# A new order of all steps, 29 copies and residual sums on another engine, and new buffers in a four-layer attention kernel

## The chip, the cores and the metric

The kernel runs on one core of a Trainium2 chip. The metric is the device time of one execution in microseconds. A core has five engines that run side by side, each through its own list of instructions in order: PE (TensorE, matmuls, with the weight loads shown apart as PEld), DVE (VectorE), ACT (ScalarE), POOL (GpSimd) and SP (SyncE, which here issues nearly all transfers). An instruction waits until what it reads is written and until the buffer that it writes is free.

## The reference

A residual stream x of 2048 x 512 (bf16) goes through four layers, A, B, A, B. The two A layers share their weights, and so do the two B layers. 32 heads of 16.

```python
def _A_ref(x, wqkv, w_phi, wo):
    q, k, v = qkv[0], qkv[1], qkv[2]              # qkv = x @ wqkv, by head
    pq = jnp.einsum("bhsd,hdf->bhsf", q, w_phi)
    pk = jnp.einsum("bhsd,hdf->bhsf", k, w_phi)
    phi_q = jnp.concatenate([_softmax(pq), _softmax(-pq)], axis=-1)
    phi_k = jnp.concatenate([_softmax(pk), _softmax(-pk)], axis=-1)
    kv = jnp.einsum("bhsf,bhsd->bhfd", phi_k, v)
    z  = jnp.einsum("bhsf->bhf", phi_k)
    num = jnp.einsum("bhqf,bhfd->bhqd", phi_q, kv)
    den = jnp.einsum("bhqf,bhf->bhq", phi_q, z)[..., None] + 1e-6
    return merge_heads(num / den) @ wo

def _B_ref(x, wqkv, wo):                          # W, dil = 8, 2
    idx = pos[:, None] - off[None, :]             # off = 0, 2, .. 14
    logits = jnp.einsum("bhsd,bhswd->bhsw", q, kg) * scale   # kg, vg: k, v at idx
    logits = jnp.where(mask, logits, -1e9)        # mask = idx >= 0
    return merge_heads(einsum(softmax(logits), vg)) @ wo

x = x + _A_ref(_layernorm(x), A_wqkv, A_w_phi, A_wo)
x = x + _B_ref(_layernorm(x), B_wqkv, B_wo)
x = x + _A_ref(_layernorm(x), A_wqkv, A_w_phi, A_wo)
x = x + _B_ref(_layernorm(x), B_wqkv, B_wo)
```

## The kernel before

x stays on the core as four blocks (x0 to x3) of 512 rows, each four tiles of 128x512. A stage is a piece of a layer on one block: `a1_01v` is the v part of stage a1 in layer 0 on block 1, `b3_13o` the output projection of the second B layer (its pass is numbered 1) on block 3. Each stage puts its steps on lists, one list for each engine. When all lists stand, `run()` goes through the table `_ORDER`, 1492 base-36 numbers, each the number of a list, and each time issues the next step of that list. So the table is the program order, and with it the order on every engine; nothing reorders it later, and the waits between the engines are put in from what each step reads and writes.

Two more tables are read on the way. `_CHOICE` has one bit for each step that can run on either of two engines (a *flex* step): a copy from PSUM runs on DVE with 1 and on ACT with 0; the layernorm apply on DVE (L466) with 1 and on ACT (L468) with 0; a residual sum with 0 on DVE (L571), and with 1 as one more matmul by the identity on PE (L556) and a pass of ACT (L568) that moves the sum to x. `_SLOTS` gives every temporary its buffer: 8 PSUM banks (ps), 14 medium, 8 big and 6 small ones.

In order of time:

- The start. SP loads the four tiles of x0 one by one (L337), the other blocks whole (L340), the raw q and k weights in halves (L349), v's weights (L343) and the output weights (L353). PE first runs 14 warm-up matmuls on zeros (L309), which can stand between others. The q and k weights are folded with w_phi: transposes (L386), copies wT (L202 on DVE, L204 on ACT), matmuls (L396), copies to WA. The first layernorm: statistics (L515, L516), factor (L450, L453, nmr L457), apply xn (L466 or L468), transposes (L482 on PE, L473 as a DMA), copies xnT.
- A layers. a1: k by matmuls (L632) and exponentials Ek (L638), v (L644), the sums and reciprocals of the softmax (L665 to L685, L690), kv (L707). a2: q (L737), exponentials Eq (L745), sums (L753). akv: kv to PE's layout (kvT, L783, L792, L796 writes R). a3: the denominator by matmuls (L821), s (L829), Ds (L832), logarithm and exponential on ACT (L835, L836), rho (L840 on DVE), which is spread over partitions by matmuls (L847, copied to bs by ACT at L886 or read directly) and multiplied into Eq (L855). a4: output by matmuls (L940). Then the output projection (L553) and the residual.
- B layers. b1: q, k, v (L967), copies, gathers Vg (L1028). b2: products of q and shifted k on DVE (L1059), sums by matmuls (L1066), exponentials (L1073). b3: weighted values (L1121, L1128), projection (L553), residual. The last B block that is started, early enough to overlap others, goes by bands (e1 to e4): projections (L1185, L1200), queries by transfers Qbd (L1240), values stored to DRAM (L1246, L1249) and read back shifted as WA and Vx (L1257), scores (L1292), exponentials (L1313), values (L1336), transposes (L1380).
- The stores of x (L582) and a check of the bounds that the fast path assumes (L1402 to L1429).

Of the kernel before, what the change touches and what calls it, by code (L numbers as in the profile page):

```python
# [65 lines left out]
2a 2k 2f 2n 2k 3a 2o 2j 24 2q 2r 2q 2o 2o 2o 29 2y 28 2y 2y 3c 2l 2z 2v 2z 2s 2z 2z 2k 2y 2z 39 36 31 2z 36 2z
3a 3b 36 36 2v 31 2v 37 2v 31 2t 36 2z 36 2b 2b 2b 2b 2m 2m ci 36 36 2m 3a 2w 2m 2v 33 34 32 31 3c 35 2q 3c 36
3b 2x g 2x 2u 2x 30 37 2x 36 38 38 38 38 3i 3c 3h 3c 39 3b 3a 3j 3k 3k 3k 3c 3d 3c 3e 3l 3b 3m 3d 3e 5h 3n 3m
3c 3e 3e 3l 5i 3m 3q 3m 3m 4f 3m 3d 3l 5j 3e 3e 3m 5i 3m 3m 3v 3d 3e 3e bd 5h 5m 5n 5i 5i 5i 3m 3d 3e 7c 5h 7d
5p 5i 5i 5i 5r 3f 3g 3g 5i 3f 3g 5i 3w 3f 3z 3x 3f 3g 5s 3y 7e 40 41 3g 7d 5u 5v 7f 5t 3g 3p 41 42 41 41 44 3g  # L70
43 3g 43 5w 5x 5x 7f 45 46 43 43 47 43 7f 5y 3f 90 47 48 49 3g 4c 91 5x 41 4b 41 41 41 4a 92 5x 4d 60 91 4l 5z
61 5z 93 5z 4q 62 5z 4g 7d 4g 4g 4m 4q 63 ck 5z 7d 4r 93 4i 4l 63 66 64 67 7g 4s 7j 65 7h 7i 4h 4j 7k bo 4n 4q
4q 4u 4w 91 7l 4t 7l 7l 7m 7l 7o 68 7n 7n 4l 7p 3h 7n 7q 4w 93 4v 7n 4v 3o 91 4f 6a 7r 4o 6b 7n 6k 6f 69 4g 4k
4l 7r 6l 7s h 4w 6g 6k 6m 4p 6a 6c 6p 7t 7u 6a 6k 6f 6n 7v 4w 6k 6h 94 6r 6d 4x 4x b2 6r 4x 97 6o 98 4x 95 6f
69 7x 96 99 99 9a 4y 6i 99 7w 9b 6q 9c 6q 9d 9b 9b 99 9e 9b 6r 6a 6e 6f 6j 83 84 d4 6q 7y 9f 7y 9b 6r 6s 6s 6s
6s 9f 9h 9i 4y 9g 4w 8d 80 9j 7z 6t 6t 3t 88 6s 83 89 6t 88 88 88 8a 8b 8f 8c 7y 6r 7x 4x 9l 6u 9k 6u 4y 6u 4w
6q 6u 83 85 83 86 87 81 9r 9w 7y 9w 9s 9x 4v 82 4v 9w 6v 9y 9z 4z a1 6v 4z 6v 6w 4z 8e 6v 4z 6y 9m 6x 6z 70 9n
70 70 71 72 73 70 9m 74 72 72 8e 9m 50 50 50 75 50 9o 72 51 9r 52 76 53 8f 54 55 72 9p 9w 76 8f 79 55 77 7a 9r
9t 55 58 78 7b 9u 55 9r 56 9m 8f 59 8g 57 5a 57 8e 8g a3 8g 8g 57 bz b0 8e 9q 57 9v a0 5b 57 8h a3 5b bz 8h a3
8g 5d c0 5e 5c 5f c0 c0 b0 c0 bz 8h b1 5g b3 b1 8f b0 b1 b3 a2 b1 a4 c0 b1 a4 b1 a3 a4 a2 a4 b4 b5 a5 bz a5 8i  # L80
# [2045 lines left out]
```

## Time and profile before

| | |
|---|---|
| median of 3 runs | 319.59 us (319.44 to 320.06) |
| span of the profiled execution | 318.1 us |
| own time of the profiled execution | not given apart from its span; the median is 1.5 us above the span |
| PE busy | 307.7 us, 97% |
| DVE busy | 295.6 us, 93% |
| ACT busy | 275.0 us, 86% |
| granted clock of PE | 1.00 |

Times in the views are microseconds from the start of the span. A row of the timeline has start, duration, engine, line, operation, written and read tiles, shape, count and, in brackets, how long the engine stood idle before it and what ended that. A row of the chain that ended last has start, length and the engine, tile and line that it is put down to. SPq is SP's queue, where transfers are issued.

### The profile page before, as it was taken

The page shows a single profiled execution, that of the slowest core. Times are in us where ns is not written, and L with a number is a line of the kernel's source. Part 1 is how long each engine was busy: PE and PEld are TensorE (multiplying, and loading weights), DVE is VectorE, ACT ScalarE, POOL GpSimd, SP SyncE. Part 2 cuts the span into 40 slices and gives each one's busy share as a digit, 9 for nine tenths or more (in the row PEclk, how much of TensorE's full clock was granted, in tenths as well). Part 3 has the DMA queues.
Part 4 walks back from the last instruction along what each step waited for, and adds up shares of the span by engine and source line. Part 5 has one row for each costly group of instructions (what it writes and reads, how often), then busy time and mean ns, then how long its engine had stood idle before and what let it go on. Part 6 is the DMA issues. An engine that isn't in the chain of part 4 may idle for free.

```text
span 318.1 us, 8900 instructions
## 1 busy us (share of the span) xinstructions
PE 307.7 (97%) x3578; PEld 152.9 (48%) x3578; DVE 295.6 (93%) x459; ACT 275.0 (86%) x639; POOL 47.2 (15%) x60
## 2 busy tenths in 40 slices
PE   8999999899999999999999999989999999999994
PEld 4644456445454444444444455544444544444552
DVE  6999996998999999999999999689998999999994
ACT  4999999999898778999999999899999867697751
POOL 6000000000004212000000000033141644045000
PEclk9999999999999999999999999999999999999999
DMA  7977100005794989939894600004289875565664
GB/s 203 358 186 148 36 2 4 2 19 145 165 178 100 156 141 136 144 66 140 145 134 62 69 0 2 4 19 134 59 185 137 140 133 134 105 178 126 158 152 170
DMA packets 45789, 36.37 MB, mean 114 GB/s; under 512 B 30832, under 2 KB 41136, under 8 KB 45744
## 3 DMA queue, kind: packets, MB, share of 16 engines
q1 hardware_dynamic: 45216, 35.75, 56.3%
q8 instruction: 29, 0.48, 0.7%
q14 instruction: 16, 0.13, 0.2%
q10 hardware_dynamic: 528, 0.02, 0.1%
HBM read 11.13 MB, written 3.25 MB: 45 GB/s over the span
## 4 chain that ended last, share of the span: by engine, by line
PE 87%; DVE 5%; ACT 5%; DMA 1%; issue 1%; SPq 0%; DVEq 0%; ACTq 0%
PE PS L967 23%; PE PS L553 18%; PE PS L632 9%; PE PS L644 9%; PE PS L737 6%; PE PS L1128 4%; PE PS L1066 4%; PE PS L1185 2%; DVE Eq L855 2%; PE PS L707 2%; PE PS L940 1%; PE PS L482 1%; PE PS L556 1%; PE PS L1200 1%; PE PS L1082 1%; DMA x<-in_A_x_dram 1%
## 5 line engine op out<-in xcount | busy, mean ns | idle before, releaser
L967 PE MATMUL PS<-xnT,WB 128*128 128x512 bf16 x336 | 76.8, 380 | 0.1
L1059 DVE TENSOR_TENSOR prod<-QT,K 128x4096 bf16<-128x4096 bf16 x28 | 63.4, 2287 | 0.5 <-POOL K L993 0.5
L1121 DVE TENSOR_TENSOR pav<-PT,Vg 128x4096 bf16<-128x4096 bf16 (+1 forms) x29 | 62.9, 2214 | 0.2
L967 PEld LDWEIGHTS <-WB 128*128 128x128 bf16 x336 | 37.3, 114 | 36.4 <-issue 3.3
L745 ACT ACTIVATE Eq<-PS 128x512 bf16<-128x512 f32 x64 | 36.3, 619 | 0.0
L638 ACT ACTIVATE Ek<-PS 128x512 bf16<-128x512 f32 x64 | 35.1, 622 | 0.2 <-PE PS L632 0.2
L553 PEld LDWEIGHTS <-oT 128*128 128x128 bf16 x236 | 21.9, 98 | 26.6 <-issue 1.3
L737 PE MATMUL PS<-xnT,WA 128*128 128x512 bf16 x128 | 32.0, 380 | 0.5 <-DVE s L829 0.3
L578 ACT ACTIVATE sqd<-x 128x512 bf16<-128x512 bf16 x48 | 29.9, 631 | 2.2 <-DVE x L571 2.0
L644 PE MATMUL PS<-WA,xnT 128*128 128x512 bf16 x128 | 31.6, 379 | 0.0
L632 PE MATMUL PS<-WA,xnT 128*128 128x512 bf16 x128 | 31.0, 379 | 0.2 <-ACT WA L204 0.2
L571 DVE SCALAR_TENSOR_TENSOR x<-PS,x 128x512 bf16<-128x512 f32 x46 | 30.2, 684 | 0.7 <-PE PS L553 0.7
L204 ACT CAST oT<-PS 128x512 bf16<-128x512 f32 (+1 forms) x50 | 26.7, 597 | 3.8 <-PE PS L1128 2.1
L553 PE MATMUL PS<-WoA,oT 128*128 128x512 bf16 x128 | 29.8, 380 | 0.0
L553 PE MATMUL PS<-WoB,oT 128*128 128x512 bf16 x108 | 26.5, 379 | 0.0
L204 ACT CAST K<-PS 128x512 bf16<-128x512 f32 x30 | 17.3, 593 | 3.1 <-PE PS L967 1.9
L632 PEld LDWEIGHTS <-xnT 128*128 128x128 bf16 x128 | 12.3, 98 | 15.2 <-issue 1.0
L644 PEld LDWEIGHTS <-xnT 128*128 128x128 bf16 x128 | 12.2, 98 | 14.5 <-issue 0.4
L690 DVE TENSOR_TENSOR Ek<-Ek,rk 128x4096 bf16<-128x4096 bf16 (+1 forms) x10 | 18.6, 1860 | 0.4 <-ACT rk L685 0.4
L737 PEld LDWEIGHTS <-WA 128*128 128x128 bf16 x128 | 11.6, 98 | 14.6 <-issue 1.7
L466 DVE TENSOR_SCALAR xn<-x,rstd,nmr 128x512 bf16<-128x512 bf16 x48 | 18.1, 424 | 0.6
L204 ACT CAST V<-PS 128x512 bf16<-128x512 f32 x26 | 15.2, 596 | 2.6 <-PE PS L967 2.6
(175 smaller groups left out, 505.1 us busy)
## 6 DMA issues: line engine op xcount, KB each, us to landing
Vg<-V SPq DMA_DIRECT2D x112, 131.5 KB, 4.3
Prho<-rd SPq DMA_DIRECT2D x8, 512.0 KB, 6.1
x<-in_A_x_dram SPq DMA_DIRECT2D x3, 512.0 KB, 6.6
WB<-in_B_wqkv_dram SPq DMA_DIRECT2D x3, 512.0 KB, 9.8
out_dram<-x SPq DMA_DIRECT2D x6, 256.0 KB, 2.3
wraw<-in_A_wqkv_dram SPq DMA_DIRECT2D x4, 256.0 KB, 4.5
vd<-Vs SPq DMA_DIRECT2D x2, 272.0 KB, 2.9
x<-in_A_x_dram SPq DMA_DIRECT2D x4, 128.0 KB, 3.4
```

The source lines that it names most:

```text
L204: self.nc.scalar.copy(out=out, in_=in_)
L553: nc.tensor.matmul(y[:], lhsT=lh(t, c), rhs=Wo()[:, c, :], start=(c == 0), stop=(c == NB - 1 and not onpe))
L571: nc.vector.scalar_tensor_tensor(out=xb[:, t, :], in0=T[t][:], scalar=1.0, in1=xb[:, t, :], op0=ALU.mult, op1=ALU.add, **kw)
L578: nc.scalar.activation(out=sqd[:], in_=xb[:, t, :], func=ACT.Square, accum_out=T["ss"][:, t:t + 1])
L632: nc.tensor.matmul(pk[:], lhsT=xnT[:, t, k, :], rhs=self.WA[:, k, D:2 * D], start=(k == 0), stop=(k == NB - 1))
L638: nc.scalar.activation(out=T["E"][:, t, s, :], in_=T["k", t][:], func=ACT.Exp, scale=1.0 - 2.0 * s)
L644: nc.tensor.matmul(pv[:], lhsT=xnT[:, t, k, :], rhs=self.WA[:, k, 2 * D:3 * D], start=(k == 0), stop=(k == NB - 1))
L737: nc.tensor.matmul(pq[:], lhsT=self.WA[:, k, hb * P:(hb + 1) * P], rhs=xnT[:, :, k, :], start=(k == 0), stop=(k == NB - 1))
L745: nc.scalar.activation(out=self.Eq[L, b][s][:, :, hb, :], in_=T[hb][:].rearrange("p (t i) -> p t i", t=4), func=ACT.Exp, scale=1.0 - 2.0 * s)
L967: nc.tensor.matmul(pp[:], lhsT=self.WB[:, k, i * D + c:(i + 1) * D:NB], rhs=xnT[:, :, k, :], start=(k == 0), stop=(k == NB - 1))
L1059: nc.vector.tensor_tensor(out=pr[:], in0=QT[:, c:c + 1, :].to_broadcast([P, NW, TB]), in1=win, op=ALU.mult)
L1121: nc.vector.tensor_tensor(out=pv, in0=PT[:, :, lo:lo + n].unsqueeze(1).to_broadcast([P, NB, 2, n]), in1=vw, op=ALU.mult)
```

## The change

All of `_ORDER` and of `_SLOTS` is written anew, and 29 bits of `_CHOICE` are turned. Nothing else differs: the steps, their shapes and the arithmetic are the same. The 29 bits, by stage, function and tile (1 is DVE for a copy `ev` and an apply `ap`, 1 is PE and ACT for a residual `res`):

```
lnA001 ap1 1->0    a1_00v ev2 0->1   a1_01v ev1 1->0   a1_02v ev3 1->0   a1_03v ev3 0->1
b1_00q ev(0,2) 1->0   b1_00k ev(1,2) 1->0   b3_00o res0 0->1   a4_01o ap0 0->1   b3_01o ap0 0->1
a4_02o ap0 1->0   a4_02o ap2 1->0   a1_12v ev2 0->1   a1_13v ev1 1->0   a1_13v ev2 0->1
b1_10k ev(1,0) 0->1   b1_10v ev(2,2) 1->0   b1_10v ev(2,3) 1->0   b3_10o res3 0->1   a4_11 ev2 1->0
a4_11o res1 1->0   b1_11k ev(1,3) 1->0   b3_11o res3 1->0   a4_12o ap3 0->1   a4_13 ev0 1->0
a4_13 ev2 0->1   a4_13 ev3 0->1   a4_13o ap3 0->1   b3_13o res2 0->1
```

A line of the diff of each table, as a sample:

```diff
 _ORDER = """
-8 2 i 2e 3s e3 ce 2p 23 i a 5l i i 9 i i i 5o i i i i 4e e7 1m i 0 3u 3r 0 f i e c j b 2 k 3 4 j o 5q 1m l 3 m
+0 2 2 8 i 2p 0 3 i 4 a i e i i i i i f 3 c 9 1m i 0 7 j k b i j o i l 1 p 1m 1n o m 1t i 6 1o 1m i n 1u z z 1m q
...
 _CHOICE = (
-    "0010111110111111101111100001000000000111010010000111011110010100001100111010001000000000011011111100"
+    "0000111110111111101111100001000000010101010000001111011110010100001100111000000000000000111011111100"
...
```

What this makes of the engines' own lists is shown at three places.

SP at the start: the first transfers, before and then now (x_83 is x0, x_84 to x_86 are x1 to x3).

```order
L349 DMA wraw<-in_A_wqkv_dram 128x4x256
L337 DMA x_83<-in_A_x_dram 128x512 x2
L349 DMA wraw<-in_A_wqkv_dram 128x4x256 x2
L340 DMA x_84<-in_A_x_dram 128x4x512
L349 DMA wraw<-in_A_wqkv_dram 128x4x256
L337 DMA x_83<-in_A_x_dram 128x512
L343 DMA WA<-in_A_wqkv_dram 128x4x512
```
```order
L337 DMA x_83<-in_A_x_dram 128x512
L349 DMA wraw<-in_A_wqkv_dram 128x4x256 x2
L337 DMA x_83<-in_A_x_dram 128x512
L349 DMA wraw<-in_A_wqkv_dram 128x4x256
L340 DMA x_84<-in_A_x_dram 128x4x512
L349 DMA wraw<-in_A_wqkv_dram 128x4x256
L337 DMA x_83<-in_A_x_dram 128x512
L353 DMA WoA<-in_A_wo_dram 32x4x512
```

The first tile of x0 moved ahead of all, and the second tile behind both halves of one weight instead of behind one half.

ACT at the start, from the copy of the first transposed tile on, before and then now.

```order
L204 CAST WA<-PS 128x512
L204 COPY xnT<-PS 128x512
L204 CAST WA<-PS 128x512 x3
L204 COPY wT<-PS 128x1024
L638 ACTIVATE Ek<-PS 128x512
```
```order
L468 ACTIVATE xn<-x_83,nmr,rstd 128x512
L204 CAST WA<-PS 128x512 x4
L204 COPY xnT<-PS 128x512
L204 COPY wT<-PS 128x1024
L638 ACTIVATE Ek<-PS 128x512
```

The apply of the second tile of x0 (it stood on DVE, as its first L466) is new here, ahead of the four copies of folded weights, and the copy of that tile's transpose moved behind them.

DVE where the first layer's normaliser is made, before and then now.

```order
L796 TENSOR_TENSOR R<-PS,mask_98 128x256
L829 TENSOR_TENSOR s_1086<-PS,rS 128x256
L832 TENSOR_TENSOR Ds<-s_1086 128x128
L840 TENSOR_TENSOR rho<-rS,Ds 128x256
L829 TENSOR_TENSOR s_1153<-PS,rS 128x256
L832 TENSOR_TENSOR Ds<-s_1153 128x128
L855 TENSOR_TENSOR Eq<-PS,Eq 128x512 x2
L855 TENSOR_TENSOR Eq<-bs,Eq 128x512
L855 TENSOR_TENSOR Eq<-PS,Eq 128x512 x2
L840 TENSOR_TENSOR rho<-rS,Ds 128x256
L855 TENSOR_TENSOR Eq<-PS,Eq 128x512 x4
```
```order
L829 TENSOR_TENSOR s_1127<-PS,rS 128x256
L832 TENSOR_TENSOR Ds<-s_1127 128x128
L796 TENSOR_TENSOR R<-PS,mask_98 128x256
L840 TENSOR_TENSOR rho<-rS,Ds 128x256
L829 TENSOR_TENSOR s_1156<-PS,rS 128x256
L832 TENSOR_TENSOR Ds<-s_1156 128x128
L855 TENSOR_TENSOR Eq<-PS,Eq 128x512 x2
L855 TENSOR_TENSOR Eq<-bs,Eq 128x512
L855 TENSOR_TENSOR Eq<-PS,Eq 128x512
L840 TENSOR_TENSOR rho<-rS,Ds 128x256
L855 TENSOR_TENSOR Eq<-PS,Eq 128x512 x5
```

R moved behind the first two links, and the second rho ahead of one product of the five that stood before it.

On PE's list, the 14 warm-up matmuls stood as 11, 2 and 1 between the first transposes; now they stand as 8, 3, 1, 1 and 1, the last one behind the eighth matmul of the first k projection. PE has 13555 rows now (weight loads counted) where it had 13553: one residual matmul more, with its weights.

More of the change, by code (lines that the diff above doesn't have):

```diff
@@ L66 @@
[L66 to L80, printed above, removed]
@@ new lines @@
+1m 1m z 1p r 1q 1r 1s z s t 1t 1v 21 22 21 1t 24 10 z i 1t 0 1w 22 t 11 5 24 13 22 12 12 u 16 1t 22 t 15 v 1t 14
+12 1x x 1z 1y 18 12 w w y 2c 18 18 2d 2d 2c 21 24 25 2d 18 17 39 22 19 26 2c 27 18 1f 3a 2e 39 3a 21 22 1b d 2d
+1c 2f 2d 1a 3a 1d 1f 2c 39 2f 3a 1f 3b 22 22 2d 1f 2d 2f 2g 1e 3a 2n 2d 1g 29 3a 1f 29 2q 3c 1h 2n 2h 2n 1i 1j
+2o 30 2q 29 29 2n 1k 2k 20 2o 2i 2k 2o 2k 24 2a 2r 2q 2k 2o 1l 29 2o 2o 2o 2y 2o 28 2l 2y 2t 2z 2f 3b g 2z 3c 2z
+2v 2y 2k 2z 2y 36 2z 2z 31 36 36 23 2z 36 2j 31 37 3c 39 2b 2z 2v 2b 2v 31 7 20 2q 2s 3b 33 36 2v 36 31 3a 2w 2b
@@ new lines @@
+20 32 34 2b 2u 2m 36 36 3c 3a 2m 2m h 2m 36 2v 2x 35 37 2x 3c 2x 2x 36 3c 38 38 38 38 3i 39 3b 3h 3a 3j 3c 3k 3d
+3c 3k 3l 3b 5h 3e 3d bo 3e 4f 3c 3d 3m 3n 3k 3e b2 20 3m 3l 3r 3o 5i 3e 3m 3l 7 3q 3e 3d 3s 3p 3m 5j 3t 3m 3m 3v
+3e 4e 3e 5i 3u 5h 5k 3e 3m 5m 3d 7 7c 3m 5n 5i d4 5h 3e 5l 3f 5i 5q 3m 5i 3f 5p 5o 5r 3g 3g 3m 7d 3g 5i 20 3w 3g
+3f 3x 5i 3z 5i 5i 3f 3g 5i 5s 3g 3y 40 41 5t 5v 41 7e 5w 3g 42 5u 7d 41 44 45 41 5x 3g 46 43 3f 90 43 5x 43 43
+47 5y 43 7f 47 48 5x 3g 41 49 41 4c 7f 4b 91 4a 41 41 4d 61 92 5x 5z 4g 60 62 91 5z 7f 5z 4l 93 4h 5z 4q 4g 4g
@@ new lines @@
+4l 93 4i 7d 63 7d 4q 4r 5z 7g 4m 4q 7k 63 67 64 4q 7j 65 66 4l 7i 68 7h 4s 4l 4n 4u 7l 93 7l 4w 4t 7l 4o 7l 91
+7m 6k 4f 6k 4g 3h 7o 4j 6f 7n 7n 7p 6l 7q 7n 6k 4w 7n 7r 6m 6a 91 7n 6k 4p 6a 7r 6a 6g 6n 69 7t 6f 4k 4w 6o 7v
+6p 6b 4v 94 4w 6c 4x 7u 4v 6h 6r 6r 96 6q 4x 4x 4x 98 95 97 20 7s 99 99 99 99 9a 69 6f 9c 4y 6d 7w 9d 6a 6f 6q
+7y 9b 9b 9e 6i 83 9b 6e 9b 6r 6j 9f 8d 6r 9b 7y 9f 7z 80 6s 9j 6q 6s 9i 6s 84 9h 9g 6s 4y 7x 88 6t 8f 6t 6s 83
+88 9k 4w 6t 83 6q 7y 4x 20 88 6r 8a 9r 89 9w 9w 6u 6u 85 6u 8b 81 9w 4v 9x 7y 88 83 4y 4w 6u 4z 86 6v 9y 8c 6v
@@ new lines @@
+4z 6v 82 87 9s 4v 6v 4z 6w a1 6y 8e 6x 6z 9m 4z 70 70 70 9n 9z 70 71 9m 72 73 9m 50 72 50 74 50 75 50 9r 72 7x
+72 9o 76 9p 8f 9r 52 72 53 51 54 9t 76 55 55 79 8f bd 77 55 7a 78 56 55 9m 58 57 59 9r 8f 8g 8e 5a 57 a3 9u 57
+57 9v 5b 8g 9q 7b 8g 8g 9w a3 8h 8h 57 5b bz 9l a3 bz a0 5f 8g c0 5e 8e c0 5d c0 8h b0 b3 5c c0 bz b0 b0 b1 8e
+c0 b1 b1 5g a2 c0 a2 b3 a4 8f a3 a4 b1 b1 b5 b1 a4 a4 a5 bz b3 b4 bx a5 8i a4 c0 b6 bx b3 bx bx by a5 b0 by by
+8j c0 b7 a2 8i 8i a3 by by by 8j 8i a6 8j by 8j ap ap ar b1 8k 8m 8l 8n 8o by 8o aq a6 8o aq 8p aq 8o b1 aq as
@@ new lines @@
+8r 8q 8s as 8q 8t a2 ap 8q 8q a6 ap as bz au 8u iw at 8q 8u a6 aq a7 aq a7 8w aq 8y 8v a7 a8 bx aq aa a7 8x as
+a9 ab b8 ax ac 8z b8 c6 ad aw ac ac ac b8 ax be b8 av by af c0 ae bb c1 b9 ae ag bf ae ah b8 be ae bb bc ai bc
+ae bc ax ax ai bb aj bb ak bc bc bc ac d3 ac am ac an bc bc ay bg ac al be ao bm bm bm bn c1 bm bn bn bj ax bn
+bu be bu az az az az bu bu c2 bj c2 bn bj ba bn ba ba bv c1 bu bp c1 bn c2 bn bj bp bi bu bp bu bk bu c2 bu bp
+c2 bj bh bs bq ba bv br i7 bl bu bt bl bl c2 bl c2 bw bw bw bw c2 ix c7 c1 c2 c8 c9 c9 c9 ca cb fp iw c3 cc c4
@@ new lines @@
+cb fq ca cd c4 ca cf cg cb ce ch ci fr ck cb cb c3 c3 cb cj cb fq cb e0 cb c4 c4 c4 c3 c4 c4 cb c5 fs cl fs e1
+c4 cm e2 cn e1 c3 e0 cp co fs c5 e4 cq e5 e3 e6 e1 e0 e1 e1 cq e7 c4 e8 cq e9 e1 ea e1 e1 e1 e1 eb h9 cr ct fq
+ef ec cq ed fq ee cs cv cs eg cu cs eh ft ha cs eg fx fu fv eg hb cw ha fw cs eg ei fy el fy cw ej hc d1 hc fy
+cx cy cq d0 ek cq cq cq d2 ei fz fy g3 hc cz ei df d5 df ei g0 em g1 df ei df em eq da dg di eo en ep dh ha dj
+d6 g2 db er ha g0 da g0 dk d5 g0 g4 d5 hd dc d5 hg hh dk dl da he hf hi hi hj hi hi et hl ey d9 d7 ey hm et g0
@@ new lines @@
+dk et hn g4 g7 dd hk f3 hk hk hk ho hk g6 g8 ez ho da hq hp g5 hs eu d8 hr dl f3 ht i7 de dm f3 dl ev f4 f3 f6
+dl g9 i1 d4 ey dk ew f7 i1 dm dm f0 es dm f5 f8 i9 f1 es i2 fa i3 ey i1 i6 fa i6 et f9 i6 fa hu f9 dn dn i9 dl
+dm f2 ex i6 fb ga i6 fb i4 c6 gq fa fb dn dl i6 i6 fb do do i1 fc i9 hv f9 gl fc ia ib gg i6 fb i9 i5 gm do hw
+i6 ic hu id dp i6 i6 fc ie dp i6 i8 fa dp ds c5 ic fd gb hw gh gb i6 i6 i6 gl i6 gg ic dq hx f9 gl fd do hw gc
+ic gn dr gg hy ic gd ic ic hw gi ic go fd dp fe fe ic hz fe i0 dt if ff fg if ic gg ig ic ig gb gk gj gs ge if
@@ L101 @@
+if ic gl gb ig ic fh gs gs if gt gt ig gt if ih gp gf ic ig du ig gs if ig if ic du ih ig gt ii ih gr dv gu ij
+ii fd gu ij ij gr ih ij du gt dy gr du gu ik il ik ii gr dw gs dz fe il dx fi fj ij im fj fj iq dx in gv ij gv
+ik fk fl fj iq fm fn ir gv ii is ij ij gw ik gw il gw fo il gv io gx iq ip iq gv gz iv fm gy it iu h2 gw iy it
+gw h0 h2 h3 h1 h3 ga h2 h4 h6 h3 h2 h5 h7 h3 h5 iz h5 h8 iy h5 j0
 """
 _CHOICE = (
-    "0010111110111111101111100001000000000111010010000111011110010100001100111010001000000000011011111100"
@@ L109 @@
+    "0000000011111110000000001000100110011011010110111010100001000000000001011110010000001000011100000000"
+    "00000000010000101000001110000000000000000000000011000010110000000000000000001110"
 )
```

50 lines of the change are left out of this document (12 added, 38 removed).

## The prediction

> **What bounds the kernel now.** I read the head of the page first, then the share of each engine on the chain that ended last, then a table of the busy time of each engine in stretches that I cut where PE stops being full.
>
> ```profile
> span 318.1 us, 8900 instructions
> PE 307.7 (97%) x3578; PEld 152.9 (48%) x3578; DVE 295.6 (93%) x459; ACT 275.0 (86%) x639; POOL 47.2 (15%) x60
> PE 87%; DVE 5%; ACT 5%; DMA 1%; issue 1%; SPq 0%; DVEq 0%; ACTq 0%
> ```
> ```profile
> core 0: us, PE busy (x) PEld busy (x) DVE busy (x) ACT busy (x) POOL busy (x), PEclk, DMA share, GB/s
> 0.00:16.50 16.50, 14.84 (x126) 8.79 (x127) 13.20 (x44) 11.29 (x24) 5.16 (x29) 1.00 0.91 283
> 16.50:44.00 27.50, 27.50 (x131) 12.52 (x129) 26.61 (x51) 27.28 (x59) 0.38 (x1) 1.00 0.44 99
> 44.00:63.00 19.00, 17.45 (x553) 11.05 (x552) 15.07 (x29) 18.05 (x40) 0.47 (x2) 1.00 0.01 3
> 63.00:76.00 13.00, 13.00 (x190) 6.28 (x188) 11.77 (x34) 12.39 (x30) 0.00 (x0) 1.00 0.35 90
> 76.00:203.00 127.00, 126.95 (x1089) 60.46 (x1089) 124.86 (x159) 116.47 (x275) 9.32 (x13) 1.00 0.66 104
> 203.00:221.00 18.00, 15.47 (x423) 8.48 (x414) 14.54 (x37) 16.45 (x39) 5.26 (x2) 1.00 0.25 68
> 221.00:281.00 60.00, 60.00 (x432) 28.52 (x434) 56.82 (x77) 49.79 (x118) 20.31 (x12) 1.00 0.66 124
> 281.00:308.00 27.00, 26.41 (x621) 13.88 (x614) 26.64 (x22) 21.19 (x56) 6.27 (x2) 1.00 0.69 167
> 308.00:318.10 10.10, 6.06 (x46) 2.93 (x45) 6.03 (x15) 2.12 (x6) 0.00 (x0) 1.00 0.39 135
> ```
>
> PE is 97% busy and 87% of the chain. In the table the first number after the stretch is its length and the next is PE's busy time. In four stretches (16.5 to 44, 63 to 76, 76 to 203, 221 to 281: 227.5 us) PE is idle for 0.05 us together. A new order can't gain there, whatever it does on DVE and ACT; it can only lose. What an order can move lies in the other five: the start (1.7 us idle), the two places where a linear layer's normaliser is made (1.55 and 2.5), the end (0.6) and the tail (4.0, where the last residual and the store run down). That is some 10 us, of which the start's first 1.3 us and most of the tail are no matter of order.
>
> **The work on PE.** A 128x512 matmul costs PE this much in a run of 48, and a residual added on PE one such matmul more:
>
> ```profile
> 88.71 10.36 PE PS L967 x48
> ...
> 289.56 0.22 PE PS L556
> ```
> ```profile
> L571 DVE SCALAR_TENSOR_TENSOR x<-PS,x 128x512 bf16<-128x512 f32 x46 | 30.2, 684 | 0.7 <-PE PS L553 0.7
> ```
>
> 10.36/48 = 0.216 us. Of the flips, three residuals go to PE (first tile of b3_00, fourth of b3_10, third of b3_13) and two come back (a4_11, b3_11), so PE gets one matmul more: +0.2 us (0 if it falls where PE waits anyway, +0.2 else). I take +0.2, since most of the five lie in stretches that are full.
>
> The same flips take work from DVE and give some to ACT: three PSUM copies fewer on DVE (28 to 25 of the flips' kind), one layernorm apply more, one residual less. By rows (0.68 us a copy on DVE, 0.58 on ACT and of an apply 0.40 and 0.81, quoted below; 0.68 a residual on DVE by the last row, and on ACT the length of a copy, an estimate) that is 3 x 0.68 + 0.68 - 0.40 = 2.3 us off DVE and 3 x 0.58 + 0.58 - 0.81 = 1.5 us onto ACT over the whole span. Hidden work: PE is full in most of the places where the 24 other flips lie, and in 76 to 203 ACT still has 10.5 us idle. I cost them at nothing, except the one at the start. If that cover is gone, each costs at most one copy, 0.6 us.
>
> **The start.** The timeline, in order of time:
>
> ```profile
> 1.34 4.53 PE L309 MATMUL PS<-kvT 128*128 128x512 bf16 x11 [1.34 <-DVE kvT L264]
> 1.42 0.98 SPq L337 DMA_DIRECT2D x<-in_A_x_dram  x2
> ...
> 6.14 0.69 DVE L515 BATCH_NORM_STATS2 stat<-x 128x6 f32<-128x512 bf16 x1
> ...
> 7.64 0.16 DVE L457 SCALAR_TENSOR_TENSOR nmr<-mv,rstd 128x1 f32<-128x1 f32 x1
> ...
> 8.32 0.40 DVE L466 TENSOR_SCALAR xn<-x,rstd,nmr 128x512 bf16<-128x512 bf16 x1
> ...
> 8.64 0.68 DVE L202 COPY wT<-PS 128x1024 bf16<-128x1024 bf16 x1
> ...
> 8.78 0.58 ACT L204 CAST WA<-PS 128x512 bf16<-128x512 f32 x1 [0.63 <-PE PS L396]
> ...
> 11.17 1.07 ACT L204 COPY wT<-PS 128x1024 bf16<-128x1024 bf16 x1
> ...
> 15.41 1.00 ACT L204 COPY xnT<-PS 128x1024 bf16<-128x1024 bf16 x1
> ...
> 16.50 1.24 PE L632 MATMUL PS<-WA,xnT 128*128 128x512 bf16 x5
> ```
> ```profile
> L468 ACT ACTIVATE xn<-x,nmr,rstd x16: 798/814/862, 6.3 to 248.8; 128x512 bf16<-128x512 bf16 x16
> ```
> ```profile
> DMA to landing us min/median/max: 3.1/3.4/3.7
> ```
> ```profile
> GB/s 203 358 186 148 36 2 4 2 19 145 165 178 100 156 141 136 144 66 140 145 134 62 69 0 2 4 19 134 59 185 137 140 133 134 105 178 126 158 152 170
> ```
>
> Before, the first two x tiles go out as SP's second and third transfer (0.98 us for two issues, so the second leaves at 1.9). Now the first tile leaves first and the second fourth, behind two weight halves: some 0.49 later, at 2.4. With the row's 3.1 to 3.7 us to landing (the row is of these four loads) it is there at 5.5 to 6.1, in time for the statistics at 6.14, which DVE reached only then. That is the low end: no delay. The high end counts the extra 256 KB ahead of it at the best rate of any slice, 358 GB/s: 0.72 us more on top, so statistics 1.2 us late. I take 0.4, nearer the low end, because the landing row already holds transfers with others ahead of them.
>
> The layernorm apply of that tile moves from DVE (0.40 us at 8.32) to ACT (0.81 by the row of L468), and on ACT it stands ahead of four weight copies. After the factor nmr (7.64 + 0.16, plus 0.4) it runs from 8.2 to 9.0; ACT's first weight copy began at 8.78 after 0.63 idle. So ACT is 0.2 to 0.3 late, and from there it has hardly a gap (27.28 of 27.50 us in the next stretch). The copies at 11.17 and 15.41 go by that, and the matmuls at 16.50 come behind the latter, with PE full from there on: **+0.3 us** (0 to +1.0, the latter with 1.2 us late). In return DVE is rid of 0.40 us, which starts its third weight copy (8.64) a little earlier; that is why I do not take more.
>
> **The first normaliser chain (44 to 63) and the second (203 to 221).** PE waits here for DVE's rho, which ACT and DVE hand to each other. The first row is the view of waits (us in total, times, longest), the others the timeline:
>
> ```profile
> PE PS L847 <- DVE rho L840: 2.6, 4, 1.0
> ```
> ```profile
> 60.53 1.88 DVE L855 TENSOR_TENSOR Eq<-PS,Eq 128x512 bf16<-128x512 f32 x3
> 60.67 0.40 PE L847 MATMUL PS<-rho,indB 32*128 32x128 bf16 x16 [0.84 <-DVE rho L840]
> ```
> ```profile
> 208.16 0.40 PE L847 MATMUL PS<-rho,indB 32*128 32x128 bf16 x16 [0.63 <-DVE rho L840]
> ...
> 214.63 0.42 DVE L840 TENSOR_TENSOR rho<-rS,Ds 128x256 bf16<-128x256 f32 x1 [0.24 <-ACT Ds L836]
> ...
> 215.11 0.41 PE L847 MATMUL PS<-rho,indB 32*128 32x128 bf16 x16 [0.95 <-DVE rho L840]
> ```
>
> In the first, the new order sets the second rho one product earlier on DVE (five products ahead of it become four), and R behind the first two links. The move is worth one product of DVE's, 1.88/3 = 0.63 us, on the wait of 0.84. But the two spreading matmul groups (L847) of a half stand closer behind one another now, and the second needs banks that ACT's copies set free: I take +0.1 for the exit of this stretch, with ends -0.4 (the product's gain comes through) and +0.5 (a copy of 0.6 in the way). In the second, the chain from the last kv matmul through ACT's copy of kvT to the first rho has the same links in the same order, so 208.16 stays; behind it the products are dealt out in another order with the same number ahead of the rho at 214.63. I take 0, with -0.9 (the 0.95 wait goes) and +0.5.
>
> **The end.** PE waits 0.5 us for the gathered values Vx, whose issues stand late in SP's queue:
>
> ```profile
> 288.56 1.84 SPq L1257 DMA_DIRECT2D Vx<-vd  x4
> ...
> 292.42 0.19 PE L1336 MATMUL PS<-Vx,et 128*32 128x68 bf16 x1 [0.50 <-DMA Vx<-vd]
> ```
>
> SP's queue there now has the query transfers and one part of the values' store in another sequence; the loads of WA and Vx still stand behind all of them and behind four of Vg. If the last store is ready sooner, the 0.5 goes; DVE, busy 26.64 of 27.00 us in that stretch, gives the next limit just behind. I take -0.1 (ends -0.5 and +0.5, the latter when a query transfer that SP now waits for comes late and holds all that is behind it).
>
> **The sum**: +0.2 +0.3 +0.1 +0 -0.1 = +0.5 us on the span of 318.1. The median of the runs shown is 319.59, 1.5 us above the span; what lies around the span is not touched, so I carry it over: 319.6 + 0.5 = 320.1 us. A measurement of this kernel tells about 0.2%, 0.64 us, from no change, so this is no change that can be told, on its upper side. Its own range is 319.4 to 320.5.
>
> **Rivals.** (1) Faster: the rho waits shorten. What speaks for it: PE's waits in 203 to 221 are 2.5 us, the products of DVE are the one thing in front of rho, and the order of both changed. What speaks against: the links of the chain and the number of products ahead of the third rho are the same. If the first chain gains 0.4, the second 0.9 and the end 0.5, with +0.5 from start and residual, it is -1.3: 318.3 us. It becomes faster than 0.2% once the waits fall by 1.2 us together. Chance 0.30.
>
> (2) Slower: the second x tile lands 1.2 us late, and since its apply stands ahead of four weight copies on ACT, all of them wait. Then the start costs +1.0 and the sum is +1.2: 320.8 us. It decides from a delay of 0.6 us on (+0.14 over my start's). For it: ACT has 0.2 us of gaps in 16.5 to 44 and 0.95 in 44 to 63, so little is made up. Against: the landing row. Chance 0.24.
>
> (3) Slower: the clock. In the row at 1.34 eleven warm-up matmuls take 4.53 us, 0.41 each, against 0.216 later; the new order has 8 of the 14 ahead of the first transposes, 8 x 0.41 = 3.3 us, where 11 stood, and then waits for a weight half. If the clock rises one such stretch later, 4.53 us in which PE is 90% busy (14.84 of 16.50) go at half speed: up to 4.53 x 0.9 / 2 = +2.0 us, 322.1 us with the rest. Against it: matmuls follow at once in the fold, and the granted clock reads 1.00 in every row of the table. Chance 0.08. [...]
>
> (4) The change does nothing because PE's full stretches swallow it: 319.6 + 0.2 for the residual. That has the same outcome as the forecast, and shares its chance, 0.38.
>
> **The numbers.** Forecast and (4) 0.38, faster 0.30, slower 0.24 + 0.08 = 0.32. The range 318.3 to 321.5 reaches to the price of rival (1) and past that of (2); it leaves out most of (3) and a tail of (1).
>
> **What would show it.** Right: a group of L468 at some 8.2 ahead of four copies of L204 on ACT; the first matmuls of L632 for the second block at 16.8; the stretches from there to the first chain and from 76 to 203 full; 18 matmuls of L556; the waits for L840 at 2.6 us together. Wrong: a sum of the waits for L840 under 1.5 us (rival 1); the second L515 beyond 6.9 (rival 2); warm-up matmuls at 0.41 beyond 6 us (rival 3); gaps in the full stretches, which would mean that a flip to ACT lost its cover.

## The result and the profile after

The changed kernel takes 324.07 us (median of 4 runs, 323.78 to 324.21), beside 319.82 us of the kernel before (4 runs). The ratio is 1.0128 (95% interval 1.0108 to 1.0149): 4.2 us slower, outside the range that was forecast. A few executions, whatever the kernel, took longer than the others (e4's traced one 453.88 us, at a granted clock of 0.66); the times below leave these out, and that trace is not read. The head of the page and the chain, after:

```profile
span 322.3 us, 8910 instructions
PE 309.1 (96%) x3579; PEld 153.5 (48%) x3579; DVE 293.3 (91%) x456; ACT 275.2 (85%) x642; POOL 48.3 (15%) x60
PE 89%; ACT 3%; DMA 2%; SPq 2%; DVE 1%; issue 1%; ACTq 0%
```

PE got the one matmul more and DVE 2.3 us less, as counted; ACT got 0.2 us more where 1.5 was counted, and PE's busy time grew by 1.4 us, of which that matmul is 0.2. The table by stretches, cut where the same work lies (columns as before):

```profile
0.00:18.00 18.00, 15.41 (x126) 9.19 (x127) 13.19 (x43) 12.24 (x25) 6.08 (x29) 1.00 0.72 213
18.00:45.00 27.00, 27.00 (x128) 12.15 (x125) 26.09 (x51) 26.22 (x57) 0.00 (x0) 1.00 0.52 123
45.00:65.00 20.00, 17.60 (x551) 11.30 (x552) 14.64 (x29) 18.66 (x40) 0.84 (x5) 1.00 0.01 3
...
80.00:205.00 125.00, 125.00 (x1063) 59.49 (x1063) 121.67 (x152) 115.51 (x275) 19.38 (x14) 1.00 0.65 108
205.00:225.00 20.00, 17.03 (x447) 9.38 (x440) 16.05 (x36) 17.41 (x41) 5.26 (x2) 1.00 0.25 62
225.00:285.00 60.00, 59.98 (x443) 28.16 (x445) 56.34 (x81) 48.18 (x116) 15.83 (x9) 1.00 0.68 137
285.00:312.00 27.00, 25.77 (x602) 13.51 (x592) 26.06 (x22) 19.36 (x54) 0.86 (x1) 1.00 0.74 138
312.00:322.30 10.30, 6.37 (x51) 3.20 (x47) 5.57 (x13) 3.28 (x8) 0.00 (x0) 0.93 0.40 134
```

The full stretches are full again. The tail reads a clock of 0.93 and is 0.2 us longer. PE's idle time grew at the start (2.6 us against 1.7), in both linear layers' middle parts (2.4 against 1.55, 3.0 against 2.5) and at the end (1.2 against 0.6). What PE waited for, by the view of waits:

```profile
PE PS L1380 <- issue: 1.2, 1, 1.2
PE PS L847 <- DVE rho L840: 1.2, 2, 0.7
PE PS L707 <- issue: 1.0, 1, 1.0
PE PS L386 <- DMA wraw<-in_A_wqkv_dram: 0.9, 2, 0.5
PE PS L753 <- issue: 0.8, 1, 0.8
PE PS L847 <- ACT Eq L745: 0.7, 1, 0.7
PE PS L847 <- DVE Eq L855: 0.6, 1, 0.6
```

The waits of the spreading matmuls (L847) are 2.5 us together, against 2.6 before, though only 1.2 us of them are now put down to rho. New are three waits put down to "issue", 3.0 us together: PE stood still and the profile knows of nothing that it waited for. Each lies inside a group of equal small matmuls. In the chain of waits and (last row) the timeline:

```profile
49.28 2.73 PE PS L707 x180
52.01 0.98 issue
53.00 0.82 PE PS L707 x44
...
299.99 1.22 issue
```
```profile
207.43 0.52 PE L753 MATMUL PS<-Eq,indS 128*32 128x128 bf16 x24 [0.77 <-issue]
```

The rest is in the first 18 us, in the timeline:

```profile
6.95 0.69 DVE L515 BATCH_NORM_STATS2 stat<-x 128x6 f32<-128x512 bf16 x1 [2.12 <-DMA x<-in_A_x_dram]
8.80 0.81 ACT L468 ACTIVATE xn<-x,nmr,rstd 128x512 bf16<-128x512 bf16 x1
9.60 2.05 ACT L204 CAST WA<-PS 128x512 bf16<-128x512 f32 x4
14.79 0.69 DVE L515 BATCH_NORM_STATS2 stat<-x 128x6 f32<-128x512 bf16 x1 [0.62 <-DMA x<-in_A_x_dram]
18.00 2.32 PE L632 MATMUL PS<-WA,xnT 128*128 128x512 bf16 x10
```

The statistics of x0's tile 1 wait for the load until 6.95 (6.14 before), the four weight copies start at 9.60 (8.78), then tile 3 waits for its load too (14.79), and the second block's k starts at 18.00 (16.50): 1.5 us. The chain comes there through SP's queue and the transfer of tile 3:

```profile
7.96 6.81 DMA x<-in_A_x_dram
```

So 1.5 + 3.0 = 4.5 us lost, 0.2 for the residual's matmul, and 0.5 us won back at the end, where the wait for Vx is gone from the view. That is the 4.2 us of the span, but the three gaps are not all net loss, since a gap also covers waits that stood beside it (the wait of 0.7 us for kvT ahead of L783 is gone as well). As far as two orders can be compared, the same matmuls show it by their starts, after and before: the first of L940 at 67.0 us (64.4), the first of L1292 at 285.4 (282.3), the last of L1336 at 309.6 (305.3). The kernel is 1.5 us behind after the start, 2.6 after the first gap, 3.1 after the second and 4.3 after the third.

### The profile page after: what moved, and what is told of

Its sections match the earlier page's. It is cut to its first block, busy times and chain, and to the rows that moved or that the text cites. A ratio compares the mean times of both kernels' runs of the same rounds, so it can differ in the third digit from the quotient of the medians.

```text
span 322.3 us, 8910 instructions
## 1 busy us (share of the span) xinstructions
PE 309.1 (96%) x3579; PEld 153.5 (48%) x3579; DVE 293.3 (91%) x456; ACT 275.2 (85%) x642; POOL 48.3 (15%) x60
## 4 chain that ended last, share of the span: by engine, by line
PE 89%; ACT 3%; DMA 2%; SPq 2%; DVE 1%; issue 1%; ACTq 0%
PE PS L967 23%; PE PS L553 17%; PE PS L644 8%; PE PS L632 8%; PE PS L737 7%; PE PS L1066 4%; PE PS L1128 4%; PE PS L707 3%; PE PS L1185 2%; DMA x<-in_A_x_dram 2%; ACT Eq L745 2%; PE PS L482 1%; PE PS L940 1%; PE PS L556 1%; PE PS L1200 1%
## 5 line engine op out<-in xcount | busy, mean ns | idle before, releaser
L745 ACT ACTIVATE Eq<-PS 128x512 bf16<-128x512 f32 x64 | 35.3, 613 | 0.3 <-PE PS L737 0.2
L578 ACT ACTIVATE sqd<-x 128x512 bf16<-128x512 bf16 x48 | 30.6, 652 | 2.7 <-DVE x L571 2.6
L571 DVE SCALAR_TENSOR_TENSOR x<-PS,x 128x512 bf16<-128x512 f32 x45 | 29.4, 683 | 2.8 <-PE PS L553 2.7
L204 ACT CAST V<-PS 128x512 bf16<-128x512 f32 x28 | 16.6, 610 | 4.9 <-PE PS L967 4.8
L204 ACT CAST K<-PS 128x512 bf16<-128x512 f32 x31 | 18.2, 599 | 2.5 <-PE PS L967 1.6
L1009 POOL COPY vh<-V 128x64 bf16<-128x64 bf16 x6 | 12.1, 2016 | 50.1 <-ACT V L204 49.3
```

Of the source, the lines that this page charges most:

```text
L204: self.nc.scalar.copy(out=out, in_=in_)
L571: nc.vector.scalar_tensor_tensor(out=xb[:, t, :], in0=T[t][:], scalar=1.0, in1=xb[:, t, :], op0=ALU.mult, op1=ALU.add, **kw)
L578: nc.scalar.activation(out=sqd[:], in_=xb[:, t, :], func=ACT.Square, accum_out=T["ss"][:, t:t + 1])
L745: nc.scalar.activation(out=self.Eq[L, b][s][:, :, hb, :], in_=T[hb][:].rearrange("p (t i) -> p t i", t=4), func=ACT.Exp, scale=1.0 - 2.0 * s)
```

## The experiments

**What the gaps are.** Two theories: PE's own program arrives late (A), or a wait that the profile does not name (B). The view of transfers has a queue of its own for instructions:

```profile
q8 instruction: 29, 0.48, 0.7%
```

29 transfers of 16.6 KB; e2 below, whose PE program is 200 instructions longer, has 30. Counting the matmuls that started ahead of each gap (column of PE, the number behind x) in the changed kernel gives 479, 2141 and 3287:

```profile
0.00:52.50 52.50, 49.42 (x479) 26.04 (x479) 45.92 (x102) 45.89 (x96) 6.08 (x29) 1.00 0.51 136
0.00:207.20 207.20, 201.66 (x2141) 100.65 (x2141) 189.91 (x308) 188.83 (x431) 26.31 (x48) 1.00 0.55 105
0.00:300.50 300.50, 291.97 (x3287) 143.97 (x3288) 277.18 (x435) 266.88 (x621) 48.26 (x60) 1.00 0.57 111
```

With a weight load each, these are instructions 958, 4282 and 6574; their distances, 3324 and 5616, are 13 x 256 - 4 and 22 x 256 - 16, and the trace has 4 and 15 semaphore instructions of PE in between, which are not counted here. So all three stand at the same place in a block of 256, to within one instruction. The transfers go by the same size: 86 matmuls have started when the first begins (14.46 us) and 3536 when the 28th does (312.86), which is 127.8 matmuls with their loads from one to the next. The 3.0 us that theory A takes for a block is an estimate from the first two gaps: 1.9 + 1.0 and 2.2 + 0.8 us from the beginning of one block to that of the next. The first three experiments try that. In e1 the kernel before is only shifted, by 64 instructions at its start:

```diff
-            nc.tensor.matmul(self.warm_ps[:], lhsT=self.kvT[:, 0:P], rhs=self.kvT[:], start=True, stop=True)
+            _warm(self, nc)   # the first 4 calls: 9 matmuls of 128x64 by 32 columns each; then as before
```

> The kernel before, with the first 4 of its 14 warm-up matmuls replaced by 36 tiny ones (128x64 by 32 columns), so that everything behind stands 64 PE instructions later in PE's program (32 pairs of weight load and matmul). Nothing else moves. Theory A (code loading): PE's program arrives in blocks of 256 instructions; a block that PE runs through in under about 3.0 us leaves it waiting for the next. In the kernel before no block is that short. With the shift two are: the one that ends at about 198 us would take 2.3 us (0.7 short) and the one that ends at about 294 us 1.5 us (1.5 short). So up to +2.2 us: 320.5 to 322.2, with gaps within groups of equal matmuls, at PE instructions that are 194 modulo 256. Rival B (the gaps of the changed kernel are waits for data or PSUM that the profile doesn't name): no such gap, 319.6 within 0.3 us.

It took 321.72 us (8 runs, 319.87 to 323.56; ratio 1.0063, 1.0035 to 1.0092). The traced run, of 321.27 us, in the chain, and the matmuls ahead of its gap:

```profile
293.32 0.41 PE PS L1336 x50
293.73 1.57 issue
295.30 0.30 PE PS L1336 x14
```
```profile
0.00:294.50 294.50, 287.92 (x3287) 144.00 (x3288) 276.11 (x433) 263.92 (x610) 47.21 (x60) 1.00 0.56 111
```

The order of the kernel before, which ran through that group, now stops in it, and at instruction 6574 as the changed kernel does. The other gap, of 0.7 us at 198 us, did not come. The start was some 0.4 us late from the padding (second k at 16.94 us). The span grew by 1.4 us (319.5 against 318.1), so the gap cost about 1.0 net: the wait of 0.5 us for Vx that stood there is gone.

In e2 the changed kernel is shifted by 200 in the same way.

> The changed kernel, shifted by 200 PE instructions in the same manner (its first 8 warm-up matmuls replaced by 108 tiny ones). Theory A: the short block that now ends at 207 us is cut so that it takes 2.9 us, and the gap of 0.8 us there goes to 0.1; the gap at 52 us stays at about 1 us, since a run of 448 small instructions holds a whole block whatever the shift; the late one at 300 us sits elsewhere or goes. So -0.8 to -2.0 us against the changed kernel: 322.1 to 323.3. Rival B: the gaps stay at the same matmuls of the same groups, 324.1 within 0.3 us. If the tiny matmuls delay the start, both come later by that, which the first matmul of line 632 shows.

It took 324.46 us (4 runs; 1.0141, 1.0121 to 1.0162), no gain, where theory A expected 322.1 to 323.3. The second block's k came at 18.80 us, 0.8 us late from the padding; the gaps behaved as theory A has it. That at 207 us is gone, the others moved:

```profile
0.00:53.90 53.90, 50.41 (x607) 29.75 (x607) 46.10 (x102) 46.47 (x96) 6.07 (x29) 1.00 0.51 133
0.00:301.80 301.80, 293.45 (x3415) 147.70 (x3416) 278.07 (x435) 266.98 (x621) 50.06 (x60) 1.00 0.59 111
```

607 and 3415 matmuls are 128 more than 479 and 3287: just one block on, though the shift was 100 matmuls. The gaps keep to the block and not to the work. Why the time did not fall is known in part: PE's matmuls, 0.8 us late from the start, come 1.9 us late at the second kv run (L707 starts at 205.83, 203.94 in the changed kernel), some of it a wait of 0.24 us for a transfer (xnT) at 122.27 that the changed kernel does not have; that took what the missing gap gave. In e3 the order alone is edited: in the changed kernel's `_ORDER` six kv steps go ahead of the four steps with large matmuls.

```diff
 PE a1_00 kv(1)
+PE a1_00 kv(2), kv(3); a1_01 kv(0), kv(1), kv(2), kv(3)
 PE a1_03v mv(2); a1_02v mv(3); a2_01 mq(2); a1_03v mv(3)
-PE a1_00 kv(2), kv(3); a1_01 kv(0), kv(1), kv(2), kv(3)
 PE a1_02 kv(0) ...
```

> The changed kernel, with six kv groups of the first layer (a1_00's last two and a1_01's four, 96 small matmuls of line 707) issued ahead of the 16 large matmuls in front of them and not behind; every buffer stays with its step. 128 + 96 small matmuls in a row become 32 + 96, 16 large ones, and 128, as in the kernel before. Theory A: no block of 256 instructions lies within small matmuls alone, so the gap of 1.0 us at 52 us goes and the time falls by 0.5 to 1.0 us, to 323.1 to 323.6 (less than 1.0 if DVE's product for the last kv groups, which ends at 51.97, is the next limit). Rival B: the gap at the same matmul stays, 324.1 within 0.3 us.

322.83 us (4 runs; 1.0092, 1.0075 to 1.0109): 1.2 us less, more than the 0.5 to 1.0 expected. In the timeline of PE the gap at 52 us is gone and what is left there is a wait for DVE:

```profile
50.85 1.58 PE L707 MATMUL PS<-Ek,vaug 128*33 128x64 bf16 x96
52.84 0.65 PE L707 MATMUL PS<-Ek,vaug 128*33 128x64 bf16 x32 [0.41 <-DVE Ek L690]
```

The other two stayed at matmuls 2141 and 3287, but the one at 3287 was 0.7 us in this run where it had been 1.2. Theory A stands as to where the gaps are, and B falls.

**The start.** Theory C: the late loads of x0. Rival D: the apply that moved to ACT. In e4 the changed kernel's SP steps at the start are put in the order of the kernel before, up to x0.3 (x0.1 is tile 1 of x0, k.0 the first half of the raw k weights).

```diff
-SP x0.0, k.0, k.1, x0.1, q.0, x1, q.1, x0.2, wo, v, x3, x0.3, x2
+SP k.0, x0.0, x0.1, k.1, q.0, x1, q.1, x0.2, v, x0.3, wo, x3, x2
```

> The changed kernel, with the loads at the start issued in the order of the kernel before (first half of the k weights, x0's tiles 0 and 1, second half, first half of q, x1, second half, x0's tile 2, v, x0's tile 3, then one part of the output weights, x3, x2). The apply of x0's tile 1 stays on ACT. Theory C (the 1.5 us at the start are the late loads of x0's tiles 1 and 3): the statistics of tile 1 begin at 6.2 and not 6.95, the first matmul of the second block's k at 16.5 to 17.2 and not 18.0, and the time falls by 0.8 to 1.5 us: 322.6 to 323.3. Rival D (it is the apply that moved to ACT): the matmul stays at 17.7 or later, -0.3 us at most, 323.8 or more.

323.26 us (4 runs, 322.42 to 325.15; 1.0101, 1.0082 to 1.0120), 0.3% better than the changed kernel's 1.0128, at the low end of C. So e5 repeats it on top of e3, and e6 also puts the apply back on DVE.

```diff
-ACT lnA001 ap(1)   # ahead of fold1 ev2(0)
+DVE lnA001 ap(1)   # ahead of lnA010 stat(0)
```

> The changed kernel with both edits: kv groups split by the 16 large matmuls, and the loads at the start in the order of the kernel before. If the two parts are independent, they add: 324.07 - 1.24 (the split alone) - 0.8 to 1.4 (the loads) = 321.4 to 322.0. Theory C (the late loads of x0's tiles cost the start): the second block's first k matmul at 16.5 to 17.2, not 18.0 to 18.2. Rival D (the apply on ACT): 17.7 or later, and the time not under 322.5.

> As e5_after_split_loads, and the apply of x0's tile 1 back on DVE, ahead of the statistics of x1, as in the kernel before. Theory C: with the loads early the apply on ACT costs little, 0 to -0.3 us against e5. Rival D: it is the larger part, -0.6 to -1.2 us against e5.

e5: 322.23 us (4 runs; 1.0068, 1.0043 to 1.0093), a little over the 321.4 to 322.0 of the sum; e6: 322.41 us (4 runs; 1.0075, 1.0052 to 1.0098). The second block's k, in e5 and in e6:

```profile
17.02 1.67 PE L632 MATMUL PS<-WA,xnT 128*128 128x512 bf16 x7
```
```profile
16.83 1.89 PE L632 MATMUL PS<-WA,xnT 128*128 128x512 bf16 x8
```

The loads bring it from 18.0 to 17.0; the apply gives 0.2 us there and nothing in the time. That 0.2 is no difference: e7 and e10 below are one kernel, with the start of e6, and read 16.95 and 17.38. The plainest test is e8: the kernel before, with SP's loads alone in the changed kernel's order.

```diff
-SP k.0, x0.0, x0.1, k.1, q.0, x1, q.1, x0.2, v, x0.3, x2, wo, x3
+SP x0.0, k.0, k.1, x0.1, q.0, x1, q.1, x0.2, wo, v, x3, x0.3, x2
```

> The kernel before, with only SP's loads at the start in the order of the changed kernel; every other engine's list is as before. Theory C: the statistics of x0's tile 1 begin at about 6.95 and not 6.14, those of tile 3 wait for their load, the second block's first k matmul comes at 17.2 to 17.9 and not 16.5, and the time is 320.3 to 321.2 (+0.7 to +1.4). Rival D (the loads are hidden, the apply on ACT makes the start late): 319.6 to 319.9.

321.11 us (10 runs; 1.0032, 1.0018 to 1.0047), 1.0 us lost by these transfers in another order. Its timeline differs from what was expected in one point:

```profile
6.19 0.69 DVE L515 BATCH_NORM_STATS2 stat<-x 128x6 f32<-128x512 bf16 x1 [1.32 <-DMA x<-in_A_x_dram]
...
14.23 0.69 DVE L515 BATCH_NORM_STATS2 stat<-x 128x6 f32<-128x512 bf16 x1 [0.56 <-DMA x<-in_A_x_dram]
...
17.66 1.03 PE L632 MATMUL PS<-WA,xnT 128*128 128x512 bf16 x4
```

Tile 1 is there in time in this run (6.19); it is tile 3, which now stands behind one part of the output weights and all of x3 beside what it stood behind before, that makes the second k 1.2 us late. C holds, by tile 3. In the four traces with this order of the loads (the changed kernel, e2, e3, e8) the statistics of tile 1 start at 6.03 to 6.95 us, while those of tile 3 wait for their load in all of them (14.23 to 15.59), and the chain of the changed kernel goes through tile 3 as well. PE also waits for raw weights there (0.9 us in the changed kernel, 0.6 in e8); what each adds, the runs do not part.

**The second gap**, at 207 us. e7 moves one q group into the second layer's kv run, on top of e6.

```diff
-PE a2_12 mq(3)
 PE a1_13v mv(1); mv(2); mv(3); a1_11 kv(3); a1_12 kv(0); kv(1)
+PE a2_12 mq(3)
 PE a1_12 kv(2) ...
```

> As e6_after_split_loads_ap, and in the second A layer the fourth q matmul group of block 2 (4 large matmuls) is issued behind the second of the eight kv groups of blocks 2 and 3, not ahead of them, so that the block of 256 PE instructions which ends at about 205 us takes 2.9 us and not 2.1. Theory A: the gap of 0.8 to 0.9 us within line 753 goes, and the time falls by 0.5 to 0.8 us against e6. Rival B: the gap stays or something else of that length takes its place: 0.

321.97 us (6 runs; 1.0063, 1.0044 to 1.0081). The wait within L753, in e6 and then in e7:

```profile
PE PS L753 <- issue: 0.8, 1, 0.8
```
```profile
PE PS L753 <- issue: 0.2, 1, 0.2
```

The gap went as theory A has it; the time moved by 0.4 us, less than the intervals can tell. The two traces differ in the last gap too, which e7 has (1.0 us) and e6 has not.

**The gap at the end.** The block that ends there is not short: PE goes through it in 4.3 us in e6, without a gap, and in 4.4 us in the changed kernel, which then stops for 1.2. So a short block does not explain this gap. What differs is when the next block's transfer starts. In the transfers' records it starts 0.9 us behind the block boundary in e6 (at 294.87 us) and 2.3 behind it in the changed kernel (297.86), and it takes some 1.5 us in both. That this transfer is late is shown; what makes it late is the question of e9. The traffic differs. From 294 to 300 us, before and then after (the last columns are clock, share of the transfer engines, GB/s):

```profile
294.00:300.00 6.00, 6.00 (x131) 3.37 (x127) 5.64 (x7) 4.98 (x17) 0.00 (x0) 1.00 0.63 144
```
```profile
294.00:300.00 6.00, 5.97 (x158) 3.04 (x157) 6.00 (x8) 5.66 (x20) 0.00 (x0) 1.00 1.07 157
```

e9 leaves out half of the last block's gathers, and so half of its values, with e7 repeated beside it as e10.

```diff
-            for g in (0, 2, 1, 3):
+            for g in [nc.gpsimd.memset(half of Vg, 0)][1:] if last block and dl > 1 else (0, 2, 1, 3):
```

> As e7_after_split_loads_ap_akv1, with the second half of the last block's value gathers left out (8 of the last 16 transfers of line 1028; POOL fills that half of Vg with zeros, so that half of the last block's windows counts nothing). Theory E (the gap near 299 us in line 1380 is the code block that comes late because the gathers fill the transfer engines: their share is 1.0 or more from 292 to 300 in e7 and the changed kernel, 0.6 to 0.85 in the kernel before): the block's transfer starts 0.6 to 1.2 us after the block boundary and not 2.2, the gap goes under 0.4 us, and the time falls by 0.6 to 1.2 us against the run of e7 beside it. Rival F (the gap has to do with the matmuls around it and not with transfers): gap and time as in e7, within 0.3 us.

> The kernel of e7_after_split_loads_ap_akv1 once more, beside e9 on the same chip: 322.0 within 0.5 us, the gap in line 1380 again 0.7 to 1.3 us.

e9 took 320.99 us (10 runs; 1.0039, 1.0024 to 1.0053) and e10 320.88 us (10 runs; 1.0024, 1.0012 to 1.0035). The trace of e10 is of its slowest run (322.36 us). The gap in L1380, in e9 and in e10:

```profile
PE PS L1380 <- issue: 0.5, 1, 0.5
```
```profile
PE PS L1380 <- issue: 0.9, 1, 0.9
```

Half the gap went and no time: inconclusive. The block's transfer started 1.8 us behind the boundary in e9 (294.89) and 2.1 in e10 (296.17), and where it fell in e9 the engines were still 0.91 busy. That the gathers hold the block up is argued, not shown. e10 also tells how far two sessions on the chip can be compared: the same kernel as e7 came out 0.4% nearer to the kernel before. Only the sum of the steps is therefore safe: splitting the kv run, the loads, the apply and the q group together take the ratio from 1.0128 to 1.0063 (e7) or 1.0024 (e10).

**A better start?** e11 puts x0's first two tiles ahead of the first weight half, in the kernel before.

```diff
-SP k.0, x0.0, x0.1, k.1, q.0
+SP x0.0, x0.1, k.0, k.1, q.0
```

> The kernel before, with only the first two tiles of x0 loaded ahead of the first weight half and not behind it. Theory C (the order of the first loads sets the start): the statistics of both tiles begin some 0.5 us earlier, DVE is free for the first weight copy at 6.5 and not 6.96, and the second block's k comes 0 to 0.4 us earlier: 319.3 to 319.8. Rival G (the weight halves, now 0.9 us later, are what the start waits for): the first transposes of line 386 wait for their load and the time is 320.0 to 320.6.

319.81 us (12 runs; 0.9997, 0.9981 to 1.0012): no difference that can be told, from either side. No version here beats the kernel before.

## Why the prediction was wrong

- The forecast of the full stretches held (27.00 of 27, 125.00 of 125, 59.98 of 60 us), and with it that the flips are hidden: DVE lost 2.3 us of work and nothing came of it. The residual's 0.2 us is too small for the runs to single out.
- The normaliser chains were put at +0.1 and 0. The waits for rho and its products did stay (2.5 against 2.6 us). Rival (1) failed, though its sign came by the letter: the waits put down to L840 are 1.2 us, under 1.5, because L847 now waits as long for products that other rows name. What made those stretches longer is not in the chain.
- The start was put at +0.3 with a high end of +1.0; it was +1.5. The step that failed is the way from the loads to the start: the prediction followed only the second tile. That tile was 0.8 us late and not 0.4, beyond the 0.6 of rival (2) and with its sign (6.95). But in e8 it is in time and the second k is 1.2 us late all the same, by tile 3, which stands behind 640 KB more (wo's part and x3) in SP's queue and which no case had. The apply on ACT, which the sum charged, cost nothing that e6 could show.
- The end was put at -0.1. The wait for Vx went, as hoped (0.5 us), and a gap of 1.2 us came that no term foresaw.
- The term that was missing is PE's program. The prediction took "PE full" for "PE can't lose", and looked for waits on data. In the changed kernel PE stands still for 3.0 us at code that came late, of which at most some 2.8 stay in the starts above (1.1, 0.5 and 1.2). The page of before had it in sight: 29 instruction transfers, 3578 matmuls with as many loads, and runs of small matmuls. The changed order put 224 small kv matmuls in a row (448 instructions) where 128 and 128 stood, parted by 12 large ones. A whole block lay within them, which PE goes through in 128 x 2.73/180 = 1.9 us. In e2 one did too; 448 instructions need not hold one at every shift, as the expectation of e2 has it, since that takes 511.
- Rival (3), the clock, cost nothing that the chain shows, but its sign came: three warm-up matmuls from 5.58 us on take 0.49 us each, and eight transposes ahead of them 1.06 us, where the kernel before takes 0.61 for them.

```profile
4.73 1.06 PE L386 MATMUL PS<-ident,wraw 128*128 128x128 bf16 x8
5.58 1.47 PE L309 MATMUL PS<-kvT 128*128 128x512 bf16 x3
```

PE runs slow until some 6.9 us here and some 5.7 before, while the column of the clock reads 1.00 in both; that a clock makes it slow, as rival (3) has it, no run shows. The next transposes end at 7.50, and DVE, which waits for tile 1 until 6.95, starts their copy at 7.78, so the slow stretch is hidden in this run.

The traces show the block of 256 by 0.48 MB in 29 transfers, 127.8 matmuls with their loads to each, and gaps that moved by exactly 128 matmuls in e2. Most blocks cost PE nothing: in the changed kernel three of the 29 transfers go with a gap, of 1.0, 0.8 and 1.2 us, each within short matmuls.

## What to carry to other kernels

Before an order of steps is judged by its waits, count PE's instructions: in these runs most blocks of 256 (128 small matmuls with their weight loads) that PE passed in 1.9 to 2.3 us stopped it for 0.7 to 1.6 us at the next block, and a few large matmuls between the small ones took that away (from 1.0 us to none in e3, from 0.8 to 0.2 in e7). A wait put down to "issue" within a group of equal matmuls, at counts that differ by about a multiple of 128 (479, 2141 and 3287), was the sign of it here. A gap removed is not its length in time won, since the next wait may stand right behind it (in e3 one of 0.4 us for DVE). And a transfer that moves back in its queue is priced with all that now stands ahead of it, each tile by itself (640 KB more ahead of tile 3 and the second k 1.2 us late in e8).

## What the runs showed of the hardware

Blocks of 256 PE instructions that were passed in 1.9 and some 2.2 us left PE waiting for 0.8 to 1.0 us, so that the next block began some 3.0 us after they had begun; one passed in 2.0 us in e1, whose transfer took 1.5 us, left it waiting for 1.6. In the first of these stretches, the block's transfer is the only one; the row from 50 to 53.2 us shows it, 2.0% of 16 engines' time, or 1.0 us:

```profile
q8 instruction: 1, 0.02, 2.0%
```

It runs from 50.61 to 51.62, so it has ended 0.4 us before PE stops and 1.4 before PE goes on (53.00). At the second gap PE goes on 1.4 us after the end of the transfer too (206.07 and 207.43), in e1 as well (293.86 and 295.30), and at the third 1.8 us after it (299.38 and 301.20). The block that e1 was to pass in 2.3 us, near 198, left no gap; the last transfer ahead of that point stands at 192.47, some 5 us earlier. So in these traces a gap goes with the time at which the transfer lands, and how short a block may be is open.

The block's transfer at the end started 0.9 us behind the boundary in e6, where the share of the transfer engines was 1.01 (294 to 296 us), 1.8 in e9 at 0.91, and 2.3 in the changed kernel at 1.06 (296 to 298 us); that their share sets this is not shown. The wait changes from run to run: the gap at the end was 1.2 us in the changed kernel, 0.7 in e3, 0.9 in e5, none in e6, and 1.0 and 0.9 in e7 and e10, which are one kernel. e1, which differs from the kernel before only by its shift, spread over 319.87 to 323.56 us, where the kernel before stayed in 319.54 to 320.19 beside it (12 runs); that its gap near 294 us makes this spread is not shown.
